# Cosine-weighted attention and a low-rank mixer: q of batch 3 transposed by DMA, the attention work of batches 3 to 7 in other slots, the last output chunk cut at column 384

## The chip, the core and the metric

The kernel runs on one core of a Trainium2 chip. A core has a matrix engine (PE, whose weight loads are shown as PEld), a vector engine (DVE), a scalar engine (ACT), GpSimd (POOL) and SyncE (SP), which here only issues DMAs. Each takes its instructions in program order and waits on semaphores for the others. The metric is the device time of one launch in microseconds (us), lower is better.

## The reference

There are 8 batches, 8 heads, 576 rows and 64 columns per head; the mixer has 512 columns, rank 32 and a hidden layer of 2048.

```python
def phi(x, c, s):                       # c, s: cos and sin of pi/2 * row / 576
    r = np.maximum(x, 0.0)
    return np.concatenate([r * c, r * s], axis=-1)
q_p = phi(q, cos_w, sin_w); k_p = phi(k, cos_w, sin_w)
kv = np.einsum('bhsf,bhsd->bhfd', k_p, v)
z = np.sum(k_p, axis=2)
num = np.einsum('bhsf,bhfd->bhsd', q_p, kv)
den = np.einsum('bhsf,bhf->bhs', q_p, z)[..., None] + 1e-06
x = (num / den)                         # heads side by side: 576 x 512 per batch
h = x.transpose(0, 2, 1) @ U @ V        # mixes the 576 rows, rank 32
u = x + h.transpose(0, 2, 1)
out = u + np.maximum(u @ w_ch1, 0.0) @ w_ch2
```

## The kernel before

**Rows.** The 576 rows of a batch are four chunks of 128 (c = 0 to 3) and a tail of 64 (c = 4). The tails of two batches share a tile of 128 rows, so batches go in pairs (0,1), (2,3), (4,5), (6,7). `ORD` is the order tail, 0, 1, 2, 3.

**Slots.** The order of all work is written out by hand. The big matmuls of a pair are 72 slots. Slots 0 to 15 are `g1_main` of the even batch (the first layer: four matmuls of 512 columns and one evacuation to `hid` on ACT, L475), 16 to 31 that of the odd batch, 32 to 35 `g1_tail`, and 36 to 71 `g2_part`: nine output chunks of four slots each, 16 matmuls per chunk, after which DVE adds `u` (L528, `o_sb`) and a store is issued. Pair 0 has slots 0 to 71, pair 1 has 72 to 143, pair 2 has 144 to 215, pair 3 has 216 to 287. After slot i come the small pieces that are listed for i. A slot of four 512-column matmuls takes 0.865 us on PE, as the chain of waits shows ("1.73 PE g_ps L466 x8").

**Attention of a batch**, planned by `attention_plan(b, w)` at offsets from w:

- `loads` of k, v and q, issued on SP. `kst` has two buffers; `vst`, `qst`, `k_p`, `q_p` and `q_pT` have one.
- `v_prep` casts v; `k_prep` and `q_prep` make the cos half and the sin half of the features of each chunk (L211 where ACT does it, L213 where DVE does it). The engines are arguments.
- q is transposed, by `qtr_unit` (eight PE transposes a chunk through PSUM, L262, then one copy) for batches 2 and 3, or by `qtr_dma` (three DMA transposes issued on SP, L275 and L280) for batches 4 to 7.
- `kv_unit` at w and w+2, `x_unit` at w+4 to w+12 (matmuls L339; DVE computes the reciprocal and the product, L296, L297, L349, and frees the only "X" buffer of PSUM), `A_unit` at w+14 (L365, cast on DVE), `u_unit` at w+16 to w+20 (L382, DVE add L383), and `utr_dma` (DMA transposes of u on SP, L401 and L407) at w+18 to w+21.

The windows are w = 40, 57, 88, 124, 160, 196 for batches 2 to 7. Batch b must be through before `g1_main` of its half-pair: slot 72 for batch 2, 88 for batch 3, 144, 160, 216, 232 for the others.

```python
p0 = -26 if b % 2 == 0 and b > 2 else -14
...
put(p0 + n, k_prep, c, (A_, A_) if b == 3 else (V_, V_))
```

Tile tags with two or three PSUM buffers ("o" 2, "g" 3) are lent to the small pieces by `spare`: "o" in the first 36 slots of a pair, where `g1` runs, "g" in the last 36.

**The last chunk** (pair 3, cc = 8) is cut into two halves of 256 columns in one PSUM tile, each with its own add and store on SP. Stores of the other pairs are issued on POOL.

Of the kernel before, what the change touches and what calls it, by code (L numbers as in the profile page):

```python
# [17 lines left out]
def kernel(  # L18
# [11 lines left out]
    nc = tc.nc  # L30

    B = 8
    H = 8
# [4 lines left out]
    DM = 512  # L38
    DH = 2048
    R = 32  # L40
    NJ = DH // P
    NPAIR = B // 2
# [19 lines left out]
    def alloc_k(b):  # L62
        kst[b] = pool.tile([P, H, 4, D], FP32, tag="kst", bufs=2, name="kst")
        kt[b] = pool.tile([P, H, D], FP32, tag="kt", bufs=2, name="kt")

    def alloc_v(b):
        vst[b] = pool.tile([P, H, 4, D], FP32, tag="vst", bufs=1, name="vst")
        vt[b] = pool.tile([P, H, D], FP32, tag="vt", bufs=1, name="vt")

    def alloc_q(b):  # L70
        qst[b] = pool.tile([P, H, 4, D], FP32, tag="qst", bufs=1, name="qst")
        qt[b] = pool.tile([P, H, D], FP32, tag="qt", bufs=1, name="qt")

    def load_main(dst, src, b, h0=0, h1=H, eng=None):
        (eng or nc.sync).dma_start(
            out=dst[:, h0:h1, :, :].rearrange("p h c d -> p h (c d)"),
            in_=src[b, h0:h1, 0:512, :].rearrange("h (p c) d -> p h (c d)", c=4),
        )

    def load_tail(dst, src, b, eng=None):  # L80
        (eng or nc.sync).dma_start(
            out=dst[tail(b), :, :],
            in_=src[b, :, 512:S, :].rearrange("h s d -> s h d"),
        )
# [23 lines left out]
    V_, A_, G_ = nc.vector, nc.scalar, nc.gpsimd  # L108
# [391 lines left out]
    def g2_part(pr, cc, part):  # L500

        last = pr == NPAIR - 1 and cc == 8
        if part == 0:
            o_ps[pr, cc] = ps.tile([P, DM], FP32, tag="o", bufs=2, name="o_ps")
        o = o_ps[pr, cc]
        if cc == 4:
            b, lhs, c, u = None, hid_tl[pr], 0, u_tl[pr]
        else:
            b, c = (2 * pr, cc) if cc < 4 else (2 * pr + 1, cc - 5)
            lhs, u = hid[b], u_bf[b][:, c, :]  # L510

        if last:
            cols, js = slice(part // 2 * 256, part // 2 * 256 + 256), part % 2 * 8
            js = range(js, js + 8)
        else:
            cols, js = slice(0, DM), range(part * 4, part * 4 + 4)
        for j in js:
            nc.tensor.matmul(  # L518
                out=o[:, cols],
                lhsT=lhs[:, j, c * P : c * P + P],  # L520
                rhs=w2_bf[:, j, cols],
                start=(j == 0),
                stop=(j == NJ - 1),
            )
        if js[-1] < NJ - 1:
            return
        o_sb = pool.tile([P, DM], FP32, tag="o_sb", bufs=3, name="o_sb")
        nc.vector.tensor_tensor(  # L528
            out=o_sb[:, cols], in0=u[:, cols], in1=o[:, cols], op=ALU.add
        )  # L530
        eng = nc.sync if pr == NPAIR - 1 else nc.gpsimd
        if cc == 4:
            for i in range(2):
                eng.dma_start(
                    out=out[2 * pr + i, 512:S, :], in_=o_sb[i * TS : i * TS + TS, :]
                )
        else:
            eng.dma_start(  # L538
                out=out[b, 0:512, cols].rearrange("(p c) n -> p c n", c=4)[:, c, :],
                in_=o_sb[:, cols],  # L540
            )


    def loads(b, eng):
        def kk():
            alloc_k(b)
            load_tail(kt[b], k, b, eng)
            load_main(kst[b], k, b, eng=eng)

        def vv():  # L550
            alloc_v(b)
            load_tail(vt[b], v, b, eng)
            load_main(vst[b], v, b, eng=eng)

        def qq():
            alloc_q(b)
            load_tail(qt[b], q, b, eng)
            load_main(qst[b], q, b, eng=eng)

        return kk, vv, qq  # L560

    ORD = (4, 0, 1, 2, 3)

    Q_BY_DMA = (4, 5, 6, 7)

    def spare(at):

        return ("o", 2) if at % 72 < 36 else ("g", 3)

    def attention_plan(b, w):  # L570

        plan = []

        def put(at, f, *a, tag=False):
            if tag:
                a = a + spare(w + at)
            plan.append((w + at, lambda: f(b, *a)))

        p0 = -26 if b % 2 == 0 and b > 2 else -14
        for n, c in enumerate(ORD):  # L580
            at = {2: -21, 3: -20}.get(b, p0 - 1)
            put(at + n, v_prep, 0, H, (c,), (G_ if b == 2 else A_,))
        for n, c in enumerate(ORD):
            put(p0 + n, k_prep, c, (A_, A_) if b == 3 else (V_, V_))
            if b in (2, 3):
                put(p0 + n, q_prep, c, (V_, A_))
            else:
                put(p0 + n, q_prep, c, (A_, None))
                put(p0 + n + 1, q_prep, c, (None, A_))
            if b not in Q_BY_DMA:  # L590
                ev = A_ if b in (2, 3) and n % 2 == 0 else V_
                put(-9 + 2 * n, qtr_unit, c, 0, H, ev)
        lo = {2: (-20, -15, -7), 3: (-13, -12, -7)}.get(b)
        if b in Q_BY_DMA:
            q0 = {4: -9, 6: -14}.get(b, p0 + 4)
            for n, (c0, c1) in enumerate(((0, 2), (2, 4), (4, 5))):
                put(q0 + 2 * n, qtr_dma, c0, c1)
            lo = (q0 + 5, q0 + 6, q0 + 7)
        put(0, kv_unit, 0, tag=True)
        put(2, kv_unit, 1, tag=True)  # L600
        for n, c in enumerate(range(5) if b in Q_BY_DMA else ORD):
            put(4 + 2 * n, x_unit, c, "X", 1)
        for n, c in enumerate(ORD):
            put(16 + n, u_unit, c, tag=True)
        put(14, A_unit, tag=True)
        if b % 2 == 1:
            put(18, utr_dma, 4, 5)
        put(19, utr_dma, 0, 2)
        put(21, utr_dma, 2, 4)
        if b + 1 < B:  # L610
            for at, t in zip(lo, loads(b + 1, nc.sync)):
                plan.append((w + at, t))
        return plan


# [120 lines left out]
    for pr in range(NPAIR):  # L736
        e, o = 2 * pr, 2 * pr + 1
        slots += [
            (lambda: None) if pr == 0 and 8 <= j < 13 else lambda j=j, e=e: g1_main(e, j)
            for j in range(NJ)  # L740
        ]
        slots += [lambda j=j, o=o: g1_main(o, j) for j in range(NJ)]
        slots += [lambda j=j, pr=pr: g1_tail(pr, j) for j in range(4)]
        slots += [
            lambda cc=cc, p=p, pr=pr: g2_part(pr, cc, p) for cc in range(9) for p in range(4)
        ]
# [3 lines left out]
    def put(at, thunk):  # L750
        todo.setdefault(at, []).append(thunk)
# [3 lines left out]
        put(18 + n, lambda b=b, c=c: u_unit(b, c, *spare(18)))  # L755
    for n, t in enumerate(loads(2, nc.sync)):
        put((11, 12, 12)[n], t)
    for b, w in ((2, 40), (3, 57), (4, 88), (5, 124), (6, 160), (7, 196)):
        for at, t in attention_plan(b, w):
            put(at, t)  # L760
    for i, s in enumerate(slots):
        s()
# [32 lines left out]
```

## Time and profile before

| | |
|---|---|
| median of 6 runs | 331.53 us (330.36 to 333.31) |
| the profiled execution: its time, its span | 330.84 us, 329.1 us |
| PE busy | 313.9 us, 95% of the span |
| ACT, DVE, POOL busy | 163.4, 151.9, 30.4 us |
| PE busy from 86 to 92 us | 3.49 of 6 us |
| PE busy from 110 to 116 us | 4.39 of 6 us |
| TensorE clock granted | 1.00 throughout |
| DMA | 50.73 MB, 154 GB/s in the mean |

A matmul's end in the trace is modelled and a running stream overlaps, so the distance between starts says more than the busy time: 216 ns for 512 columns. Where a group has one instruction fewer than the code issues (x7 for x8), its record is missing; the time is not. The stall ahead of a matmul is thus its start, less the start before it, less what the earlier one takes.

### The profile page before, as it was taken

How to read it: one execution, taken by the hardware profiler on the slowest of the kernel's cores; microseconds unless marked ns; L12 is line 12 of the kernel's file. 1: busy time of each engine (PE TensorE's matmuls, PEld its weight loads, DVE VectorE, ACT ScalarE, POOL GpSimd, SP SyncE). 2: the span in 40 equal slices, each digit the busy share in tenths (PEclk: the TensorE clock that was granted, in tenths of full speed). 3: DMA queues.
4: the chain of work that ended last, by engine and by line, in shares of the span. 5: the costliest groups of instructions: out<-in, count | busy, mean ns of one | idle time of the engine just before them, and what ended most of it. 6: DMA issues, size and time to landing. Idle time of an engine off the chain costs nothing.

```text
span 329.1 us, 5804 instructions
## 1 busy us (share of the span) xinstructions
PE 313.9 (95%) x2393; PEld 169.4 (51%) x2422; DVE 151.9 (46%) x334; ACT 163.4 (50%) x272; POOL 30.4 (9%) x61
## 2 busy tenths in 40 slices
PE   8899799999789799999999999999999999999995
PEld 3665654575455344556455444556455444464443
DVE  6779645825557851255626940345626610001211
ACT  3839655877719136555901866557700067650000
POOL 1314203001010100000111100000112000000000
PEclk9999999999999999999999999999999999999999
DMA  7999999877334118951499389702552230001131
GB/s 242 305 272 265 196 269 336 248 239 234 103 120 124 57 57 196 260 186 31 112 235 358 131 216 244 258 2 53 149 136 66 80 96 2 0 2 64 64 98 64
DMA packets 79053, 50.73 MB, mean 154 GB/s; under 512 B 47187, under 2 KB 76243, under 8 KB 79027
## 3 DMA queue, kind: packets, MB, share of 16 engines
q1 hardware_dynamic: 72594, 39.09, 42.1%
q0 software_dynamic: 6432, 11.27, 13.7%
q8 instruction: 19, 0.31, 0.4%
q14 instruction: 8, 0.06, 0.1%
HBM read 36.86 MB, written 9.44 MB: 141 GB/s over the span
## 4 chain that ended last, share of the span: by engine, by line
PE 66%; DVE 5%; issue 1%; ACT 1%; DVEq 0%
PE o_ps L518 30%; PE g_ps L466 25%; PE gt_ps L486 3%; PE va_ps L382 2%; PE kv_ps L245 2%; PE x_ps L339 2%; DVE k_p L213 2%; PE a_ps L365 2%; DVE o_sb L528 1%; PE t_ps L262 1%; DVE k_tl L213 1%; DVE rec L297 0%; ACT k_p L211 0%; DVE x_bf L349 0%; DVE rec L296 0%
## 5 line engine op out<-in xcount | busy, mean ns | idle before, releaser
L466 PE MATMUL g_ps<-uT,w_bf 128*128 128x512 bf16 x512 | 118.5, 379 | 0.1
L518 PE MATMUL o_ps<-w_bf,hid 128*128 128x512 bf16 (+1 forms) x510 | 116.3, 372 | 1.4 <-DVE o_sb L528 0.5
L475 ACT ACTIVATE hid<-g_ps 128x512 bf16<-128x512 f32 x128 | 76.2, 596 | 82.8 <-PE g_ps L466 82.7
L518 PEld LDWEIGHTS <-hid 128*128 128x128 bf16 x528 | 50.0, 98 | 53.5 <-issue 1.6
L466 PEld LDWEIGHTS <-w_bf 128*128 128x128 bf16 x512 | 48.5, 98 | 54.3
L528 DVE TENSOR_TENSOR o_sb<-u_bf,o_ps 128x512 f32<-128x512 bf16 (+1 forms) x33 | 22.1, 669 | 67.8 <-PE o_ps L518 67.7
L538 POOL DMA_DIRECT2D out_dram<-o_sb x24 | 13.4, 558 | 177.3 <-DVE o_sb L528 160.2
L383 DVE TENSOR_TENSOR u_bf<-x_bf,va_ps 128x512 bf16<-128x512 bf16 x32 | 21.9, 687 | 10.2 <-PE va_ps L382 9.4
L105 DVE CAST kv<-kv_ps 128x260 bf16<-128x260 f32 x14 | 6.0, 429 | 37.2 <-PE kv_ps L245 37.2
L211 ACT ACTIVATE q_p<-qst,sinw 128x512 bf16<-128x512 f32 x29 | 20.4, 710 | 4.4 <-DMA qst<-in_q_dram 4.4
L349 DVE TENSOR_TENSOR x_bf<-x_ps,rec 128x512 bf16<-128x512 f32 x24 | 16.6, 692 | 0.8
L103 ACT ACTIVATE v_ext<-vst 128x512 bf16<-128x512 f32 (+2 forms) x23 | 14.8, 653 | 2.9 <-DMA vst<-in_v_dram 2.8
L486 PE MATMUL gt_ps<-uT_tl,w_bf 128*128 128x128 bf16 x256 | 16.1, 219 | 0.0
L486 PEld LDWEIGHTS <-w_bf 128*128 128x128 bf16 x256 | 15.1, 98 | 1.4
L518 PE MATMUL o_ps<-w_bf,hid_tl 128*128 128x512 bf16 x62 | 15.0, 379 | 0.1
L382 PE MATMUL va_ps<-A_sb,V_bf 128*128 128x512 bf16 x37 | 14.0, 379 | 0.6 <-DVE A_sb L105 0.5
L245 PEld LDWEIGHTS <-k_p 128*128 128x128 bf16 x256 | 11.3, 97 | 5.1 <-ACT k_p L211 2.0
L172 PE MATMUL w_ps<-zero 128*128 128x512 bf16 x37 | 11.8, 459 | 1.9 <-DVE halfpi L142 1.2
L245 PE MATMUL kv_ps<-v_ext,k_p 128*128 128x65 bf16 x256 | 12.1, 193 | 1.6 <-DVE v_ext L105 1.5
L339 PEld LDWEIGHTS <-q_pT 128*128 128x128 bf16 x192 | 9.1, 98 | 8.2 <-DVE x_bf L349 1.6
L213 DVE TENSOR_SCALAR k_p<-kst,cosw 128x512 bf16<-128x512 f32 x28 | 13.1, 484 | 0.1
L296 DVE TENSOR_SCALAR rec<-x_ps 128x8 f32<-128x8 f32 (+1 forms) x30 | 4.9, 165 | 17.0 <-PE x_ps L339 16.9
(100 smaller groups left out, 261.2 us busy)
## 6 DMA issues: line engine op xcount, KB each, us to landing
qst<-in_q_dram SPq DMA_DIRECT2D x8, 1024.0 KB, 8.6
kst<-in_k_dram SPq DMA_DIRECT2D x8, 1024.0 KB, 7.3
vst<-in_v_dram SPq DMA_DIRECT2D x6, 1024.0 KB, 9.2
out_dram<-o_sb POOLq DMA_DIRECT2D x24, 256.0 KB, 2.8
w_bf<-in_moe_w_ch_dram POOLq DMA_DIRECT2D x8, 512.0 KB, 10.1
vst<-in_v_dram SPq DMA_DIRECT2D x4, 512.0 KB, 7.5
out_dram<-o_sb SPq DMA_DIRECT2D x7, 256.0 KB, 2.3
qt<-in_q_dram SPq DMA_DIRECT2D x8, 128.0 KB, 8.3
```

The lines of the kernel that those rows point to most:

```text
L211: nc.scalar.activation(out=o, in_=i, func=AF.Relu, bias=0.0, scale=w)
L213: eng.tensor_scalar(out=o, in0=i, scalar1=0.0, scalar2=w, op0=ALU.max, op1=ALU.mult)
L245: nc.tensor.matmul(out=acc[:, i, :], lhsT=k_p[b][:, c, h, :] if c < 4 else k_tl[:, h, :], rhs=vx[:, c, h, :], start=(c == 0), stop=(c == 4),)
L339: nc.tensor.matmul(out=acc[:, g, i * E : i * E + E], lhsT=qT_of(b, c, h), rhs=kv_sb[b][:, h, :], start=True, stop=True,)
L349: nc.vector.tensor_tensor(out=x_of(b, c, rows).rearrange("p (g i d) -> p g i d", g=2, d=D), in0=view[:, :, :, 0:D], in1=rec[rows].unsqueez ...
L382: nc.tensor.matmul(out=va, lhsT=V_bf[:, c, :], rhs=A_sb[b], start=True, stop=True)
L383: nc.vector.tensor_tensor(out=u_bf[b][:, c, :] if c < 4 else u_tl[b // 2][rows, :], in0=x_of(b, c, rows), in1=va[rows, :], op=ALU.add,)
L466: nc.tensor.matmul(out=g_ps.rearrange("p (c t) -> p c t", c=4), lhsT=w1_bf[:, d, j * P : j * P + P], rhs=uT[b][:, :, d, :], start=(d == 0) ...
L475: nc.scalar.activation(out=hid[b][:, j, :], in_=g_ps, func=AF.Relu, bias=0.0, scale=1.0)
L486: nc.tensor.matmul(out=g_ps[:, jj, :], lhsT=w1_bf[:, d, j * P : j * P + P], rhs=uT_tl[pr][:, d, :], start=(d == 0), stop=(d == 3),)
L518: nc.tensor.matmul(out=o[:, cols], lhsT=lhs[:, j, c * P : c * P + P], rhs=w2_bf[:, j, cols], start=(j == 0), stop=(j == NJ - 1),)
L528: nc.vector.tensor_tensor(out=o_sb[:, cols], in0=u[:, cols], in1=o[:, cols], op=ALU.add)
```

## The change

`attention_plan` takes its placements from a table, `PLAN`: w, start and engine of `v_prep`, start and engines of `k_prep`, start of `q_prep`, start of the DMA transposes of q (or "tensor"), and the places at which the loads of the next batch are issued. Batch 2 stays as it was. For batch 3 the transposes of q go from PE to DMA. Batches 3 to 7 get w = 60, 98, 128, 164, 200. Batch 4 gets `v_prep` on POOL, `k_prep` on ACT 35 slots ahead of its w, `q_prep` on DVE; for batches 5 to 7 every offset stays and w moves by four slots. The last chunk becomes 384 columns (three parts) and 128 columns (one part), the latter in a PSUM tile of its own, with its store issued on ACT.

```diff
     def g2_part(pr, cc, part):
         last = pr == NPAIR - 1 and cc == 8
-        if part == 0:
+        if part == 0 or last and part == 3:
             o_ps[pr, cc] = ps.tile([P, DM], FP32, tag="o", bufs=2, name="o_ps")
...
         if last:
-            cols, js = slice(part // 2 * 256, part // 2 * 256 + 256), part % 2 * 8
-            js = range(js, js + 8)
+            cols = slice(0, 384) if part < 3 else slice(384, DM)
+            js = (range(0, 5), range(5, 10), range(10, NJ), range(NJ))[part]
...
-        eng = nc.sync if pr == NPAIR - 1 else nc.gpsimd
+        eng = nc.gpsimd if pr < NPAIR - 1 else nc.scalar if part == 3 and last else nc.sync
...
+    KA, KV = ((A_, A_),) * 5, ((V_, V_),) * 5
+    PLAN = {
+        2: (40, -21, G_, -14, KV, -14, "tensor", (-20, -15, -7)),
+        3: (60, -20, A_, -10, KA[:2] + ((V_, A_),) * 3, -15, -9, (-16, 2, 3)),
+        4: (98, -10, G_, -35, KA, -18, -12, (-7, -6, -5)),
+        5: (128, -15, A_, -14, KV, -14, -10, (-5, -4, -3)),
+        6: (164, -27, A_, -26, KV, -26, -14, (-9, -8, -7)),
+        7: (200, -15, A_, -14, KV, -14, -10, ()),
+    }
...
+        w, v_at, v_eng, k_at, k_engs, q_at, qtr, lo = PLAN[b]
...
-        p0 = -26 if b % 2 == 0 and b > 2 else -14
         for n, c in enumerate(ORD):
-            at = {2: -21, 3: -20}.get(b, p0 - 1)
-            put(at + n, v_prep, 0, H, (c,), (G_ if b == 2 else A_,))
+            put(v_at + n, v_prep, 0, H, (c,), (v_eng,))
         for n, c in enumerate(ORD):
-            put(p0 + n, k_prep, c, (A_, A_) if b == 3 else (V_, V_))
+            put(k_at + n, k_prep, c, k_engs[n])
             if b in (2, 3):
-                put(p0 + n, q_prep, c, (V_, A_))
+                put(q_at + n, q_prep, c, (V_, A_))
+            elif b == 4:
+                put(q_at + n, q_prep, c, (V_, V_))
             else:
-                put(p0 + n, q_prep, c, (A_, None))
-                put(p0 + n + 1, q_prep, c, (None, A_))
-            if b not in Q_BY_DMA:
-                ev = A_ if b in (2, 3) and n % 2 == 0 else V_
-                put(-9 + 2 * n, qtr_unit, c, 0, H, ev)
-        lo = {2: (-20, -15, -7), 3: (-13, -12, -7)}.get(b)
-        if b in Q_BY_DMA:
-            q0 = {4: -9, 6: -14}.get(b, p0 + 4)
+                put(q_at + n, q_prep, c, (A_, None))
+                put(q_at + n + 1, q_prep, c, (None, A_))
+            if qtr == "tensor":
+                put(-9 + 2 * n, qtr_unit, c, 0, H, A_ if n % 2 == 0 else V_)
+        if qtr != "tensor":
             for n, (c0, c1) in enumerate(((0, 2), (2, 4), (4, 5))):
-                put(q0 + 2 * n, qtr_dma, c0, c1)
-            lo = (q0 + 5, q0 + 6, q0 + 7)
+                put(qtr + 2 * n, qtr_dma, c0, c1)
...
-    for b, w in ((2, 40), (3, 57), (4, 88), (5, 124), (6, 160), (7, 196)):
-        for at, t in attention_plan(b, w):
+    for b in range(2, B):
+        for at, t in attention_plan(b):
             put(at, t)
```

More of the change, by code (lines that the diff above doesn't have):

```diff
@@ L562, with attention_plan @@
     ORD = (4, 0, 1, 2, 3)
-    Q_BY_DMA = (4, 5, 6, 7)
     def spare(at):
         return ("o", 2) if at % 72 < 36 else ("g", 3)
-    def attention_plan(b, w):
+    KA, KV = ((A_, A_),) * 5, ((V_, V_),) * 5
[7 more added lines that the diff above has]
+    }
+    def attention_plan(b):
         plan = []
+        w, v_at, v_eng, k_at, k_engs, q_at, qtr, lo = PLAN[b]
         def put(at, f, *a, tag=False):
@@ L577, in put @@
             plan.append((w + at, lambda: f(b, *a)))
-        p0 = -26 if b % 2 == 0 and b > 2 else -14
         for n, c in enumerate(ORD):
-            at = {2: -21, 3: -20}.get(b, p0 - 1)
-            put(at + n, v_prep, 0, H, (c,), (G_ if b == 2 else A_,))
+            put(v_at + n, v_prep, 0, H, (c,), (v_eng,))
         for n, c in enumerate(ORD):
-            put(p0 + n, k_prep, c, (A_, A_) if b == 3 else (V_, V_))
+            put(k_at + n, k_prep, c, k_engs[n])
             if b in (2, 3):
-                put(p0 + n, q_prep, c, (V_, A_))
-            else:
-                put(p0 + n, q_prep, c, (A_, None))
-                put(p0 + n + 1, q_prep, c, (None, A_))
-            if b not in Q_BY_DMA:
-                ev = A_ if b in (2, 3) and n % 2 == 0 else V_
-                put(-9 + 2 * n, qtr_unit, c, 0, H, ev)
-        lo = {2: (-20, -15, -7), 3: (-13, -12, -7)}.get(b)
-        if b in Q_BY_DMA:
-            q0 = {4: -9, 6: -14}.get(b, p0 + 4)
+                put(q_at + n, q_prep, c, (V_, A_))
+            elif b == 4:
+                put(q_at + n, q_prep, c, (V_, V_))
+            else:
+                put(q_at + n, q_prep, c, (A_, None))
[3 more added lines that the diff above has]
+        if qtr != "tensor":
             for n, (c0, c1) in enumerate(((0, 2), (2, 4), (4, 5))):
-                put(q0 + 2 * n, qtr_dma, c0, c1)
-            lo = (q0 + 5, q0 + 6, q0 + 7)
+                put(qtr + 2 * n, qtr_dma, c0, c1)
         put(0, kv_unit, 0, tag=True)
         put(2, kv_unit, 1, tag=True)
-        for n, c in enumerate(range(5) if b in Q_BY_DMA else ORD):
+        for n, c in enumerate(ORD if qtr == "tensor" else range(5)):
             put(4 + 2 * n, x_unit, c, "X", 1)
@@ L609, in attention_plan @@
         put(21, utr_dma, 2, 4)
-        if b + 1 < B:
-            for at, t in zip(lo, loads(b + 1, nc.sync)):
-                plan.append((w + at, t))
+        for at, t in zip(lo, loads(b + 1, nc.sync) if lo else ()):
+            plan.append((w + at, t))
         return plan
```

## The prediction

> **What bounds the kernel now.** I read the page first: PE is busy 95% of the span, and of the 40 slices only the first five, three near 82 to 115 us and the last one dip.
>
> ```profile
> PE 313.9 (95%) x2393; PEld 169.4 (51%) x2422; DVE 151.9 (46%) x334; ACT 163.4 (50%) x272; POOL 30.4 (9%) x61
> PE   8899799999789799999999999999999999999995
> ```
>
> So PE's stream is the kernel, and a gain is either fewer matmuls or less waiting between them. Next the chain of waits, which leaves PE from 86 to 88, at 91, and from 105 to 114 us:
>
> ```profile
> 86.01 1.22 ACT k_p L211 x2
> 87.23 0.61 ACT q_p L211
> 87.85 0.49 ACT q_tlT L103
> 88.38 0.61 PE t_ps L262 x8
> ...
> 91.08 0.70 DVE q_pT L105
> 91.82 0.61 PE t_ps L262 x8
> ...
> 111.09 1.67 DVE k_p L213 x4
> 112.75 0.59 DVE o_sb L528
> ```
>
> ACT and DVE copy the transposes of batch 3 out of the single "T" buffer late, because feature work stands before the copies in their queues; later DVE frees the single "X" buffer late, because `k_prep` of batch 4 stands between the products of batch 3. PE's timeline has the sizes:
>
> ```profile
> 86.36 0.42 PE L339 MATMUL x_ps<-kv,q_pT 128*128 128x65 bf16 x8
> 88.38 0.61 PE L262 MATMUL t_ps<-ident,q_p 128*128 128x128 bf16 x8 [1.60 <-ACT q_tlT L103]
> ...
> 111.50 1.89 PE L518 MATMUL o_ps<-w_bf,hid 128*128 128x512 bf16 x8
> 114.53 0.42 PE L339 MATMUL x_ps<-kv,q_pT 128*128 128x65 bf16 x8 [1.15 <-DVE x_bf L349]
> ...
> 323.74 1.91 PE L518 MATMUL o_ps<-w_bf,hid 128*128 128x256 bf16 x16 [0.51 <-DVE o_sb L528]
> ```
>
> A stall is the start minus the start before it minus what that group takes (0.26 us for eight of L339, 1.73 for eight of 512 columns, both from the chain). 88.38-86.36-0.26 = 1.76; likewise 1.01 at 91.82, 0.34 at 108.61, 0.62 at 111.23, and 114.53-111.50-1.73 = 1.30. Sum: **5.03 us**. One more, 0.48 at 187.23, where `u_unit` of batch 5 waits for the cast of `A_sb`.
>
> **What the Trainium skill says.** "TensorE: Matmul & The Clock Gate", Back-to-back issue gap, gives some 81 ns per matmul for a stream of weight loads and 128-column matmuls and 56 ns for an isolated one. Here 16 of `gt_ps` take 0.89 us and eight transposes 0.45: 56 ns, weight loads included, and I use that. "PSUM — Partial Sum Buffer", PSUM bank collisions, wants engines kept apart by bank, not by address; the trace agrees: at 323.74 the second half waits for DVE's read of other columns of the same tile. "DMA: Bandwidth & Descriptors", Issuing engines are not separate DMA queues, says a store from another engine saves only sequencer time; no run shown has one from ACT. "SBUF — State Buffer", Who interferes with whom, says a DVE instruction with two SBUF inputs contends with GpSimd's reads; the trace before doesn't decide that.
>
> **The change, part by part.**
>
> *Batch 3 transposed by DMA.* Removed: 5 x 8 transposes, 5 x 0.45 = -2.24 us of PE, and the stalls behind "T", 1.76 + 1.01 = -2.77. ACT also loses three copies (two of 1.0 us, one 0.58), DVE two of 0.69. Added: three transposes on SP, 1.4 to 2.3 us each to issue, landing 3.8 to 5.3 after. q features are done on DVE near 86.7 us (its queue worked through from 79 us: products 1.07, features 0.40, adds 0.6 each), so SP issues from 85 to 90 and the last lands by 95; the first `x_unit` needs them at 102. Hidden. `x_unit` of batch 2 beside `q_prep` of batch 3 waits 0.12 at most, once: +0.12.
>
> *Batch 4's k to ACT, q and v elsewhere.* DVE has only products and adds left while batch 3's `x_unit` runs (2 x 0.865 + 0.26 = 2.0 us per unit against 1.07 + 0.3): -0.34-0.62-1.30 = -2.26. Ten k halves on ACT, 6.1 us from 100.2 (when `kv_unit` of batch 3 releases `k_p`), end at 106.4; the first `hid` of slot 72 comes at 110. Five casts on POOL (612 ns each) have 20 slots; were DVE shut out all that time, 3.1 us would be spread over units with 0.6 spare each, so I take nothing, at most +1. Ten q halves on DVE (4 us) lie in slots 80 to 84, where DVE has only the `u` adds, which stand first.
>
> *Batch 3 three slots later.* A uT transpose lands 2.7 us after issue; with the last issue near 120.0 (its `u` add ends then) it is in at 122.7 and slot 88 starts at 125.3. Nothing, with 2.6 us in hand (5 before: 127.5 against 132.5).
>
> *Batches 5 to 7 four slots later, batch 4 ten.* The output chunks recur every four slots, so the 0.48 us wait of batch 5 stays. Its `u_unit`s now fall on slots 144 to 148 and take "o" (2 buffers) for "g" (3); the second waits for the add of chunk 8: about +0.26. New is a meeting: `u_unit` of batch 4 (114 to 118) now shares its slots with `k_prep` of batch 5 on DVE. With T the start of the first of these `u` matmuls, DVE needs 0.65 + 0.8 per slot and one add, so u of c = 1 is done at T+4.4 and of c = 3 at T+7.3. SP is in order: uT transpose (T+4.4), q transpose of batch 5, uT transpose (T+7.3), two q transposes, at 1.25 to 2.3 us each: `loads` of batch 6 begin at T+12.3. In the trace before they begin at 168.10:
>
> ```profile
> 168.10 0.69 SPq L81 DMA_DIRECT2D kt<-in_k_dram  x1
> ...
> 173.80 2.52 SPq L75 DMA_DIRECT2D qst<-in_q_dram  x1
> ```
>
> q lands 10.9 us after its issue, at 184.7, and ACT, already waiting for these loads, finishes features at 190.8, just ahead of the next `hid`:
>
> ```profile
> 180.70 0.63 ACT L103 ACTIVATE v_ext<-vst 128x512 bf16<-128x512 f32 x1 [2.79 <-DMA vst<-in_v_dram]
> ...
> 190.14 0.71 ACT L211 ACTIVATE q_p<-qst,sinw 128x512 bf16<-128x512 f32 x1
> 191.74 0.60 ACT L475 ACTIVATE hid<-g_ps 128x512 bf16<-128x512 f32 x1 [0.90 <-PE g_ps L466]
> ```
>
> That is 22.7 us from first issue to free ACT; after, T+35.0, and the first `hid` of pair 2 is out of PSUM at T+35.6. PE starts slot 119 at T+4.5; from 119 to 144 took 26.5 us before, 0.86 of it `u_unit`s that now come later, so slot 144 starts at T+30.2 and slot 147, which needs the buffer of slot 144 ("g" has three), at T+30.2+3x1.08+0.26 = 33.7. **New stall: +1.85 us**, between 0 (loads land 2 us sooner) and +4 (2 us later). Behind it ACT needs 0.5 to 0.6 per `hid` against 0.865 per slot and catches up.
>
> *Last chunk.* PE issues the same 16 x 512 columns. The 128-column part has its own tile, and chunk 7's buffer was free 2 us before: the gap goes, 323.74 minus the end of the first half's stream, -0.68 (the 0.51 shown counts from a modelled end). The last add covers 128 columns: 0.42 for 256 and 0.69 for 512 give 0.285, -0.13. The 384-column add (0.55) ends within the last part's 0.89. The store: the last one before took 1.8 us from issue to landing on SP; from ACT, with nothing before or behind it, I take the same, -0.3 to +0.5 at the ends. Sum -0.81.
>
> *Sum*: -2.24-2.77-2.26+0.12+0.26+1.85-0.81 = **-5.85 us**. The profiled 330.84 becomes 325.0; it lies 0.7 below the median, 331.53, which becomes 325.7.
>
> **The rivals.**
>
> *The loads are not late*, since DVE or SP needs less than I added up. For: ACT had 0.9 us spare at 191.74. Against: ACT waited 2.8 us on v there already. Then +1.85 goes: 323.8.
>
> *A removed wait returns at slot 88*: uT of batch 3 late by 5 us, where 2.6 are in hand. For: nothing else was moved so near its deadline. Against: SP has nothing else to issue then. +2.4: 328.1.
>
> *Slower: SP's in-order queue decides.* Place: slot 147. Each us by which q of batch 6 lands later than I worked out is a us of PE. For: transposes and 3.4 MB of loads now share SP behind `u_unit`; the GB/s row has its highest value, 358, in that stretch. Against: the same bytes, only shifted. It costs more than 5.85+1.66, the bound of "slower", once q lands 7.5 us later than assumed; with its 10.9 us doubled, 336.6.
>
> **How the numbers follow.** Forecast (stall at 147 of 0.5 to 4) 0.60; loads not late 0.24; slot 88, or another return of that size, 0.11; SP decides 0.05. I allow 0.7 for where the median falls among runs that differ by up to 2.95. The range reaches from the second case less that, 323.1, to just over the slot-88 case and the forecast with a stall of 4 us (327.9), 328.5. Some 0.5% (1.66 us) is what a measurement of this kernel can tell from no change: faster 0.91, same 0.04, slower 0.05.
>
> **What would show it.** Right: no PE transpose (L262) after slot 39, so 120 of the 160 are left; PE near 6 of 6 us from 80 to 115; no gap ahead of the 128-column matmuls; one gap of 1 to 3 us at the fourth `g1_main` of pair 2, released by an ACT `hid` that follows a q feature. Wrong: PE waiting at slot 88 for uT, at slot 64 for `q_pT`, gaps between the `x_unit`s of batch 3, or a last store that takes over 2.3 us.

## The result, and the profile after

The changed kernel takes 328.97 us in the median of 16 executions (326.11 to 331.62), the one before 331.76 (35 executions); the ratio is 0.990, 95% interval 0.9874 to 0.9927. That is 2.8 to 3.3 us less, where 5.85 was forecast. The profiled execution took 326.92 us, its span is 325.1. (The ratios leave out executions over 1.5% above the fastest of their kernel; the counts of clock below keep them.)

The page after: busy time of PE, its share per slice, and the granted clock, which the page before shows at 9 in all slices.

```profile
PE 312.5 (96%) x2356; PEld 167.1 (51%) x2382; DVE 151.8 (47%) x335; ACT 156.5 (48%) x261; POOL 33.2 (10%) x66
PE   8799799999999999999999979999999999999996
PEclk9999799999999999999999999999999999999999
```

The dips near 82 to 115 us are filled. Slice 24 is new, and so is a 7 in the fifth slice of the clock. PE's timeline where batch 3's `x_unit`s had waited 0.34, 0.62 and 1.30 us:

```profile
103.94 0.42 PE L339 MATMUL x_ps<-kv,q_pT 128*128 128x65 bf16 x8
104.20 1.89 PE L518 MATMUL o_ps<-w_bf,hid 128*128 128x512 bf16 x7
105.93 0.42 PE L339 MATMUL x_ps<-kv,q_pT 128*128 128x65 bf16 x8
106.19 1.89 PE L518 MATMUL o_ps<-w_bf,hid 128*128 128x512 bf16 x8
107.91 0.42 PE L339 MATMUL x_ps<-kv,q_pT 128*128 128x65 bf16 x8
```

Every distance is 0.26 or 1.73 us: no wait. The chain of waits leads through the new dip; its first line starts when SP issues the load of q of batch 6:

```profile
173.79 7.70 DMA qst<-in_q_dram
...
186.67 3.06 ACT q_p L211 x5
189.73 0.49 ACT hid L475
```

PE's timeline at the same place:

```profile
188.07 0.38 PE L382 MATMUL va_ps<-A_sb,V_bf 128*128 128x512 bf16 x1
190.26 1.02 PE L466 MATMUL g_ps<-uT,w_bf 128*128 128x512 bf16 x4 [1.82 <-ACT hid L475]
```

v and q of batch 6 land late: ACT waits 3.30 us for v and, as its last wait, 1.06 for q. Their casts and features stand on ACT before the first `hid` of pair 2, and the fourth `g1_main` waits for that `hid`: a stall of 1.98 us (start 190.26, less 188.07 of the `u` matmul before, less 0.22, from unrounded times). The end of the kernel, in the timeline:

```profile
321.32 0.55 DVE L528 TENSOR_TENSOR o_sb<-u_bf,o_ps 128x384 f32<-128x384 bf16 x1 [1.91 <-PE o_ps L518]
322.21 0.29 DVE L528 TENSOR_TENSOR o_sb<-u_bf,o_ps 128x128 f32<-128x128 bf16 x1 [0.34 <-PE o_ps L518]
322.53 0.38 ACTq L538 DMA_DIRECT2D out_dram<-o_sb  x1
```

The matmuls run through without a gap, and the adds take what was interpolated (0.55 and 0.285).

**One measure that start and chip don't touch.** Up to slot 40 the two programs do the same work, but for three casts of batch 3 that move behind it. From the first `kv_unit` matmul of batch 2 (L245, at 75.29 before and 77.24 after) to the end of the span is 253.78 us before and 247.90 after: **-5.88 us**. The 1.95 that the profile after lost ahead of it lie in a stretch that no edit touches; from 36.21 to 39.62 us its granted clock is 0.50, which accounts for some 1.7 of them. I call this distance "from slot 40" below.

### The profile page after: what moved, and what is told of

The parts are those of the page before. It is cut to its first block, busy times and chain, and to the rows that moved or that the text cites. A ratio compares the mean times of both kernels' runs of the same rounds, so it can differ in the third digit from the quotient of the medians.

```text
span 325.1 us, 5735 instructions
## 1 busy us (share of the span) xinstructions
PE 312.5 (96%) x2356; PEld 167.1 (51%) x2382; DVE 151.8 (47%) x335; ACT 156.5 (48%) x261; POOL 33.2 (10%) x66
## 4 chain that ended last, share of the span: by engine, by line
PE 80%; DMA 9%; SPq 4%; ACT 3%; DVE 2%; issue 1%
PE o_ps L518 34%; PE g_ps L466 32%; DMA kt<-in_k_dram 5%; PE gt_ps L486 4%; DMA qst<-in_q_dram 2%; PE va_ps L382 2%; SPq L81 2%; PE kv_ps L245 2%; DMA vst<-in_v_dram 2%; PE x_ps L339 2%; PE a_ps L365 2%; SPq L75 2%; ACT q_p L211 2%; PE t_ps L262 1%; DVE k_p L213 1%
## 5 line engine op out<-in xcount | busy, mean ns | idle before, releaser
L466 PE MATMUL g_ps<-uT,w_bf 128*128 128x512 bf16 x512 | 120.3, 382 | 2.0 <-ACT hid L475 1.8
L518 PE MATMUL o_ps<-w_bf,hid 128*128 128x512 bf16 (+2 forms) x513 | 117.7, 372 | 0.8
L518 PEld LDWEIGHTS <-hid 128*128 128x128 bf16 x528 | 48.9, 98 | 51.9 <-issue 0.3
L528 DVE TENSOR_TENSOR o_sb<-u_bf,o_ps 128x512 f32<-128x512 bf16 (+2 forms) x33 | 22.0, 668 | 55.4 <-PE o_ps L518 55.2
L211 ACT ACTIVATE q_p<-qst,sinw 128x512 bf16<-128x512 f32 x25 | 17.3, 711 | 3.7 <-DMA qst<-in_q_dram 3.7
L349 DVE TENSOR_TENSOR x_bf<-x_ps,rec 128x512 bf16<-128x512 f32 x24 | 16.6, 691 | 0.8
L486 PE MATMUL gt_ps<-uT_tl,w_bf 128*128 128x128 bf16 x256 | 15.8, 219 | 0.0
L245 PEld LDWEIGHTS <-k_p 128*128 128x128 bf16 x256 | 11.2, 97 | 6.2 <-ACT k_p L211 2.0
L245 PE MATMUL kv_ps<-v_ext,k_p 128*128 128x65 bf16 x256 | 12.0, 193 | 2.5 <-DVE v_ext L105 2.5
L103 ACT ACTIVATE v_ext<-vst 128x512 bf16<-128x512 f32 (+2 forms) x19 | 12.2, 659 | 3.6 <-DMA vst<-in_v_dram 3.5
L103 ACT ACTIVATE v_ext<-vt 64x512 bf16<-64x512 f32 (+1 forms) x7 | 3.7, 534 | 19.5 <-DMA vt<-in_v_dram 19.4
```

The costliest lines, as they stand in the source:

```text
L103: nc.scalar.activation(out=o, in_=i, func=AF.Copy, bias=0.0, scale=1.0)
L211: nc.scalar.activation(out=o, in_=i, func=AF.Relu, bias=0.0, scale=w)
L245: nc.tensor.matmul(out=acc[:, i, :], lhsT=k_p[b][:, c, h, :] if c < 4 else k_tl[:, h, :], rhs=vx[:, c, h, :], start=(c == 0), stop=(c == 4),)
L349: nc.vector.tensor_tensor(out=x_of(b, c, rows).rearrange("p (g i d) -> p g i d", g=2, d=D), in0=view[:, :, :, 0:D], in1=rec[rows].unsqueez ...
L466: nc.tensor.matmul(out=g_ps.rearrange("p (c t) -> p c t", c=4), lhsT=w1_bf[:, d, j * P : j * P + P], rhs=uT[b][:, :, d, :], start=(d == 0) ...
L486: nc.tensor.matmul(out=g_ps[:, jj, :], lhsT=w1_bf[:, d, j * P : j * P + P], rhs=uT_tl[pr][:, d, :], start=(d == 0), stop=(d == 3),)
```

## The experiments

Unless said otherwise each is an edit of the changed kernel, run beside the kernel before on one chip, on which before has a median of 333.1 to 333.2. The second run of the later k features and the run with q of batch 5 on PE were on another chip, where before has 332.87.

**The changed kernel again, and the one before again.** No edit.

> The changed kernel itself, unedited, beside the kernel before on one chip, to compare at an equal mean clock. Theory (the trace's -5.9 us from slot 40 on is the change, and what the medians show less is clock): 5 to 6.5 us less than before among executions of the same mean clock, and a lower mean clock on average than before. Rival (the first 40 us got slower too): 3 to 4 us less at an equal clock.

> The kernel before, unedited, for a second profile. Theory (clock drops follow the stalls of PE): where its mean clock is under 1, the low stretch lies at the start, before 45 us, or behind one of the stalls at 88 to 92 and 108 to 115 us. Rival (drops fall anywhere): elsewhere too.

Changed: 331.51 us (6 executions), ratio 0.9874 (0.9797 to 0.9951). Before: 333.23 (20 executions), ratio 0.9987 (0.9963 to 1.0011); from slot 40 it takes 253.76, the first profile within 0.02, with the same five stalls and a clock of 1.00. The changed kernel takes 251.03 from slot 40 this time, 3.13 more than in its first profile. PE's timeline shows where:

```profile
189.43 0.38 PE L382 MATMUL va_ps<-A_sb,V_bf 128*128 128x512 bf16 x1
193.07 1.02 PE L466 MATMUL g_ps<-uT,w_bf 128*128 128x512 bf16 x4 [3.26 <-ACT hid L475]
193.93 0.38 PE L382 MATMUL va_ps<-A_sb,V_bf 128*128 128x512 bf16 x1
194.15 1.66 PE L466 MATMUL g_ps<-uT,w_bf 128*128 128x512 bf16 x4
```

The stall is 3.42 us here (q of batch 6 landed 30.8 us after the first `u` matmul of batch 4, in place of 29.4), and one microsecond after it four matmuls take 1.66 us in place of 1.02. So the stall is dearer than its length: 1.44 us of the 3.13 are the longer stall, the other 1.7 the slower matmuls behind it. The windows of three profiles show when this happens. A row gives a stretch, its length, the busy time (and the instructions) of PE, PEld, DVE, ACT and POOL, the granted clock, the DMA share and GB/s. First this second profile of the changed kernel, with its stall of 3.42 us:

```profile
190.99:194.40 3.41, 1.33 (x7) 0.62 (x7) 0.05 (x1) 3.26 (x7) 0.00 (x0) 1.00 0.35 77
194.40:197.81 3.41, 3.41 (x10) 1.22 (x9) 1.32 (x2) 0.93 (x2) 0.00 (x0) 0.50 0.00 0
```

Then the run with k of batch 4 on DVE (below), whose stall there is 2.28 us:

```profile
188.11:191.53 3.42, 1.30 (x7) 0.52 (x6) 1.42 (x3) 3.42 (x7) 0.16 (x1) 1.00 0.60 165
191.53:194.94 3.41, 3.41 (x10) 1.17 (x9) 0.69 (x1) 1.30 (x3) 0.00 (x0) 0.50 0.12 27
```

And the run with q of batch 3 on PE (below), whose stall is 3.55 us and which has no low stretch behind it:

```profile
190.70:194.11 3.41, 1.63 (x7) 0.58 (x6) 2.34 (x4) 3.41 (x7) 0.54 (x1) 1.00 0.38 115
194.11:197.53 3.42, 1.67 (x8) 0.77 (x8) 0.39 (x1) 3.26 (x6) 0.00 (x0) 1.00 0.34 77
197.53:200.94 3.41, 3.41 (x18) 1.56 (x16) 0.99 (x2) 1.92 (x4) 0.00 (x0) 1.00 0.28 65
```

In each of the twelve profiles the changes of the clock lie whole multiples of 3.413 us apart (in this second profile at 37.39, 40.80, 194.40 and 197.81; from 37.39 to 194.40 it is 46 times 3.413), a grid whose place differs from one execution to the next. What goes with a low stretch is not how long the stall is but how much of it falls into one window of that grid. Behind slot 40, up to the output's last chunk, the clock fell to 0.50 after the three windows in which PE was idle for 2.08, 2.09 and 2.12 us, and after none with less: 1.78 and 1.75 (the 3.55 us stall, cut in two by the grid), 1.51, 1.51, 1.38, 1.16, and 1.37 for the stalls behind "T" in the kernel before. (Once it stayed at 0.50 for a second window.) Ahead of slot 40 six of seven low stretches follow windows with 1.89 us of idle time or more, but one follows a window with 1.39, so this is not the whole rule. It is read from the traces; no edit moved a stall against the grid.

By mean granted clock, executions and median us:

| | 0.998 and over | 0.993 to 0.995 | 0.990 and under |
|---|---|---|---|
| before (one chip, 83) | 28: 332.0 | 49: 333.5 | 6: 335.5 |
| changed (16 + 6) | 4: 326.2 | 8: 328.8 | 10: 331.6 |
| early loads, below (6) | 2: 324.2 | 4: 326.5 | none |
| early loads, k of batch 6 on ACT, below (6) | 5: 323.4 | 1: 324.2 | none |

One low stretch, 3.41 us at half speed, loses 1.7 us, which is 0.005 of the mean clock over 330 us. So, by this estimate, the columns are executions with no low stretch, with one, and with two or more.

At an equal clock the table puts the change at 3.9 to 5.8 us, but its second row takes in the first measurement, where before is some 1.3 us faster than on the one chip. On that chip there are six executions of the changed kernel: one at full clock, 327.14 against about 332.2 (5.1 less), one at 0.995, 329.82 against 333.5 (3.7 less), and four at 0.990 and under, 332.2 against 335.5 (3.3 less). One execution bears the expectation of 5 to 6.5 out; the others lie at the rival's 3 to 4, so the rival is not excluded. The lower clock on average is there: on that chip 4 of 6 executions have lost a second stretch, against 6 of 83 before. Of the changed kernel and its edits, 27 of 69 executions of those that have the stall are at 0.990 and under, and none of the 14 of the three edits below that remove it (an execution at 0.852, below, is left out). The theory that before's drops follow its stalls got no case: neither of its profiles has a drop.

**k features of batch 5 after the u adds of batch 4, twice.**

```diff
-        5: (128, -15, A_, -14, KV, -14, -10, (-5, -4, -3)),
+        5: (128, -15, A_, -9, KV, -14, -10, (-5, -4, -3)),
```

> The changed kernel with k_prep of batch 5 five slots later (offset -9 for -14), so that DVE does the u adds of batch 4 first. Theory 1 (DVE delays u, u delays the transposes on SP, they delay the loads of batch 6, ACT is late for the hid of slot 144): loads of batch 6 begin 2.7 us sooner after the first u matmul of batch 4 (13.4 us in the changed kernel), and the stall of 1.98 us at the fourth g1_main of pair 2 falls below 0.2; 2.0 us less at an equal clock. Rival 1 (the landing of the loads is bound by what the DMA engines can move, not by when SP issues): the stall stays above 1.5. Theory 2 (that stall is also where the matrix clock drops in some executions): the median falls by clearly more than 2.0, to below 326. Rival 2 (the clock drops come from the start, which no edit touches): the median falls by 2.0, to 327.0, and runs with a mean clock of 0.99 stay as common.

> The kernel with k_prep of batch 5 five slots later once more, for a second profile and more executions. Theory (moving k_prep helps only by what SP can pass on, some 0.4 us in the first profile): the stall at the fourth g1_main of pair 2 is between 1.5 and 3.5 us again. Rival (the first profile was a disturbed one and the edit does remove the stall): below 0.5.

326.47 us (6 executions, ratio 0.9792, 0.9749 to 0.9835) and, on the other chip, 326.65 (4 executions, one of them 364.5 us at a clock of 0.852; ratio 0.9819, 0.9773 to 0.9865). The stall is not gone: 3.43 us in the first profile, which is of the slowest execution of its six (332.49), and 1.55 in the second.

```profile
164.68 2.46 SPq L280 DMA_TRANSPOSE q_tlT<-q_tl  x1
167.19 0.61 SPq L81 DMA_DIRECT2D kt<-in_k_dram  x1
```

These are SP's rows of the second. The first transpose is issued 1.5 us sooner (3.29 after the first `u` matmul of batch 4, in place of 4.81), but the last one now takes 2.46 us to issue in place of 1.25, and the loads begin at 12.8 (13.1 in the first profile) in place of 13.5 and 14.1. So of the 2.7 us I expected, 0.4 to 1.3 came through, and the order of DVE's work is not enough to remove the stall. The median is 5.0 us below the changed kernel's on the same chip (331.51) all the same: at full clock it is 325.73 against one execution at 327.14, and fewer executions are at 0.990 and under, one of six against four of six. How much of that is a shorter stall in the executions without a profile is not known.

**q of batch 5 transposed on PE.**

```diff
-        5: (128, -15, A_, -14, KV, -14, -10, (-5, -4, -3)),
+        5: (128, -15, A_, -14, KV, -14, "tensor", (-5, -4, -3)),
```

> The changed kernel with q of batch 5 transposed on PE (slots 119 to 127), so that three DMA transposes fewer stand ahead of the loads of batch 6. Theory (the transposes hold SP and the DMA engines): the loads begin near 9.2 us after the first u matmul of batch 4 (13.5 and 14.1 in the two profiles of the changed kernel), q lands near 22 (29.4 and 30.8), 12 to 13 us from first issue to landing in place of 16, and PE has no stall at the fourth g1_main of pair 2; PE itself works 2.2 us more. Rival (the loads are slow by their own bytes): 16 us from first issue to landing again, q lands at 25.

327.54 us (2 executions on the other chip, ratio 0.9846, 0.9793 to 0.9898). Loads begin at 10.0 and q lands at 25.9: 16.0 us from first issue to landing, against 15.8 and 16.6 in the changed kernel and 17.5 and 16.0 above. The rival holds: the 3.5 MB of loads took about as long without these transposes ahead of them (221 GB/s in the mean), and the transposes cost by holding SP until the loads may begin. ("tensor" also puts the tail first among this batch's `x_unit`s; the same goes for batch 3 below.) With a start 4 us sooner the stall at the fourth `g1_main` is gone. From slot 40: 247.91, the same as the changed kernel, 2.2 of PE work for 2.0 of stall.

**Loads of k and v of batch 6 ahead of those transposes.**

```diff
-        5: (128, -15, A_, -14, KV, -14, -10, (-5, -4, -3)),
+        5: (128, -15, A_, -14, KV, -14, -10, (-20, -12, -3)),
```

> The changed kernel with the loads of k and v of batch 6 issued at slots 108 and 116, ahead of the transposes, and q's after them as before. Theory (the loads of batch 6 come late because the transposes before them on the same queue fill the DMA engines; what counts is the bytes and transposes ahead, not when SP issues): q of batch 6 lands near 23 us after the first u matmul of batch 4 (29.4 in the changed kernel, 30.6 where only k_prep of batch 5 was moved), the stall at the fourth g1_main of pair 2 is below 0.2 us, 2.0 to 3.5 us less at an equal clock, and the clock drop after it is gone. Rival (k_prep of batch 5 on DVE is the cause): the stall stays above 1.5.

325.73 us, ratio 0.9761 (0.971 to 0.9813). Only q is left behind the transposes:

```profile
166.46 1.22 SPq L280 DMA_TRANSPOSE q_tlT<-q_tl  x1
168.41 0.62 SPq L75 DMA_DIRECT2D qst<-in_q_dram  x1
```

q lands 22.4 us after the first `u` matmul of batch 4 (23 expected), 6.9 sooner than in the changed kernel: 4.5 of these are an earlier issue (at 15.0 in place of 19.5), 2.4 a shorter way to landing. So when SP issues does count, other than the theory had it. The stall is gone; from slot 40: 245.92, 1.98 less than the changed kernel, which is the stall of its first profile to the last digit. And none of the 6 executions has a clock of 0.99 or less. Since `k_prep` of batch 5 stands where the change put it, the rival falls.

**And k features of batch 6 on ACT, its `v_prep` and `k_prep` seven slots sooner.**

```diff
-        6: (164, -27, A_, -26, KV, -26, -14, (-9, -8, -7)),
+        6: (164, -34, A_, -33, KA, -26, -14, (-9, -8, -7)),
```

> The same, and k_prep of batch 6 on ACT at slots 131 to 135 in place of DVE at 138 to 142. Theory: the two waits for A_sb and for the add of chunk 8 (0.49 and 0.31 us in the changed kernel) go as well, 0.8 us less than with the early loads alone. Rival (ACT has no room for ten more features): the stall at the fourth g1_main of pair 2 comes back, over 1 us.

323.54 us (322.85 to 324.19), ratio 0.9696 (0.9652 to 0.9739): the best version found, below both kernels. From slot 40: 244.99, another 0.93 less (0.8 expected, the two waits of 0.49 and 0.31), and PE has no gap over 0.24 us from slot 36 to the end:

```profile
PE   8899799999999999999999999999999999999996
```

**Parts undone: q of batch 3 on PE, k of batch 4 on DVE, the last chunk in halves.**

```diff
-        3: (60, -20, A_, -10, KA[:2] + ((V_, A_),) * 3, -15, -9, (-16, 2, 3)),
+        3: (60, -20, A_, -10, KA[:2] + ((V_, A_),) * 3, -15, "tensor", (-16, 2, 3)),
```

> The changed kernel with q of batch 3 transposed on PE again (slots 51 to 59), all features where the change put them. Theory (the stalls behind the T buffer came from features queued ahead of the copies, so the new slots alone remove most of them): 2.24 us of PE work comes back and at most 0.5 us of stalls, +2.2 to +2.7 at an equal clock. Rival (the single T buffer makes PE wait wherever the features stand): the two stalls of 2.8 us come back too, +5.0.

331.66 us (20 executions), ratio 0.9951 (0.9927 to 0.9976). From slot 40: 251.97, 4.07 more than the changed kernel's first profile; its stall at the fourth `g1_main` is 3.55, 1.57 more, which leaves +2.5. There is no gap at the five transposes; two of them, the first with its neighbours:

```profile
90.05 1.02 PE L518 MATMUL o_ps<-w_bf,hid 128*128 128x512 bf16 x4
90.91 0.61 PE L262 MATMUL t_ps<-ident,q_tl 128*128 128x128 bf16 x8
91.35 1.03 PE L518 MATMUL o_ps<-w_bf,hid_tl 128*128 128x512 bf16 x4
...
93.34 0.61 PE L262 MATMUL t_ps<-ident,q_p 128*128 128x128 bf16 x8
```

The distances are 0.86 and 0.44 us, what the matmuls take. 2.24 us of work come back, and the stalls of 2.77 do not. So the new slots of the features are enough to remove these, without the DMA transposes.

```diff
-        4: (98, -10, G_, -35, KA, -18, -12, (-7, -6, -5)),
+        4: (98, -10, G_, -35, KV, -18, -12, (-7, -6, -5)),
```

> The changed kernel with k_prep of batch 4 on DVE (slots 63 to 67) instead of ACT. Theory (the 2.26 us of stalls at x_unit of batch 3 are DVE's k features queued between the products): the gaps between the x_units return, +1.5 to +2.5 us at an equal clock. Rival (ORD against plain order, or the later slots, removed them): below +0.5.

332.88 us (12 executions), ratio 0.9991 (0.9961 to 1.0021). The stalls at `x_unit` of batch 3 are back, in PE's timeline:

```profile
107.27 0.42 PE L339 MATMUL x_ps<-kv,q_pT 128*128 128x65 bf16 x8 [0.48 <-DVE x_bf L349]
110.40 0.43 PE L339 MATMUL x_ps<-kv,q_pT 128*128 128x65 bf16 x8 [0.98 <-DVE x_bf L349]
```

0.64 and 1.14 us, +1.78 in the range expected. Its whole gain over before vanished in these executions, since 10 of 12 had a clock of 0.99 or less; in its profile the clock drops behind the stall at the fourth `g1_main`.

```diff
-        if part == 0 or last and part == 3:
+        if part == 0:
...
-            cols = slice(0, 384) if part < 3 else slice(384, DM)
-            js = (range(0, 5), range(5, 10), range(10, NJ), range(NJ))[part]
+            cols, js = slice(part // 2 * 256, part // 2 * 256 + 256), part % 2 * 8
+            js = range(js, js + 8)
...
-        eng = nc.gpsimd if pr < NPAIR - 1 else nc.scalar if part == 3 and last else nc.sync
+        eng = nc.gpsimd if pr < NPAIR - 1 else nc.sync
```

> The changed kernel with the last chunk as two halves of 256 columns in one PSUM tile, both stores on SP. Theory: +0.8 us, of it 0.68 as a gap ahead of the last sixteen matmuls and 0.13 in the last add. Rival (the store from ACT with 512-byte rows costs what the add saves): +0.5 or less.

330.09 us (6 executions), ratio 0.991 (0.9873 to 0.9947), too wide for 0.8 us. The profile decides: 249.74 from slot 40, 1.84 more, of which the stall at the fourth `g1_main` (2.90) has 0.92; the other 0.92 is the end, where the gap is back:

```profile
322.68 1.91 PE L518 MATMUL o_ps<-w_bf,hid 128*128 128x256 bf16 x16 [0.51 <-DVE o_sb L528]
```

## Why the prediction was right or wrong

- **What bounds the kernel** was right: every term was a gap or a matmul on PE, and the terms add up. From slot 40 the sum was -5.85 and the first profile has -5.88. That it is this close is in part luck: single terms are off by up to 0.13 us, and the other profile of the same kernel has 3.13 less gain. In the medians 2.8 to 3.3 us came. By the ratio that is 328.2 beside the 331.53 that the forecast started from, inside the range of 323.1 to 328.5, but near the end that was there for a long stall or a wait at slot 88. That it also held what the clock took is luck.
- **Batch 3's q: -2.24 and -2.77** are right as sums, but the second was put down to the DMA transposes alone. The stalls came from features queued before the copies, as the prediction itself says ahead of its sum; with PE transposes in the new slots they stay away too. DMA transposes with the features in their old slots were not tried. SP issued these transposes later than worked out, from 90.45 to 97.74 us with the last landing at 100.41 (85 to 90 and 95; 1.95 of this is the later start), and they were still hidden: the first of batch 3's `x_unit`s starts at 104.11.
- **Batch 4's k on ACT: -2.26** is right: no gap in the profile after, 1.78 of it back when k goes back to DVE. The five casts on POOL delayed no `x_unit`.
- **Slot 88** was met, as worked out: the last uT of batch 3 lands at 124.85 us and slot 88 starts 2.6 later. The rival of a wait returning there has no trace in the profile.
- **The new stall, +1.85**, was right in its place and its mechanism from ACT on, and 1.98 in the first profile. But its size is not a constant: seven profiles with it show 1.55 to 3.55 us, as q of batch 6 lands 28.8 to 30.9 us after the first `u` matmul of batch 4. From profile to profile the stall grows by about as much as q lands later, as the slower rival had it. The bounds of 0 to 4 held these; the middle was low for most (and 35.6 less 33.7, the prediction's own figures, is 1.9). That the first profile came so near is in part luck: the loads began at 13.5 us in place of 12.3, and from their first issue to free ACT took 21.9 us in place of 22.7. The step that named its cause was too simple: I made DVE's backlog the cause, and moving it passed on 0.4 to 1.3 of 2.7 us, because the issue of the last transpose on SP then took 2.46 and 2.99 us in place of 1.25 and 2.22.
- **What was left out** is the step that missed the median: no term for the granted clock. The page before showed 9 in all slices, so I priced a stall at its length. The Trainium skill, "TensorE: Matmul & The Clock Gate", Part 1, says that the clock is halved after an idle window of about 3.4 us that runs free of the kernel. The low stretches here do come on a grid of 3.41 us, at a clock of 0.50, but the window need not be idle throughout: PE was busy for 1.30 to 1.33 of the 3.41 us ahead of the three. So stalls of 2.28, 3.42 and 3.43 us were followed by a low stretch, and those of 1.55, 1.98, 2.90 and 3.55, cut in two by the grid, were not; before's two stalls of 1.77 and 1.01 us left at most 1.37 us idle in one window. Without the stall none of 14 executions had the second drop; of the changed kernel's 22, 10 had. That removing the stall ends the second drop is shown as far as 14 executions go; the limit between 1.78 and 2.08 us of idle time is only read off.
- **The last chunk, -0.81**: 0.92 by the part undone, 0.67 of it the gap. The store from ACT landed 1.70 us after issue, as the one from SP did (1.83).
- **The slots up to 40**, taken as unchanged, are all but unchanged in work but not in time: kv of batch 2 starts at 75.3 to 77.4 us in the five profiles with no low stretch ahead of it and at 77.2 to 79.1 in the seven with one. 49 of before's 83 executions have a low stretch's loss in their mean clock too, so it does not come with the change alone; what sets the rest of the start was not tried.

## What to carry to other kernels

Where one in-order queue issues both transposes and loads, a load's landing is set by when its turn comes plus the time of the loads themselves (16 us for q, k and v of a batch here): issue loads whose buffers are already free ahead of work that has to wait, and look whose features, on which engine, stand in front of the first evacuation of the next stage. Price a stall on the matrix engine that can leave 2 us idle within one window of 3.41 at more than its length: here the clock was halved for the next 3.41 us, which cost another 1.7. Whether it comes is a matter of chance between executions, so count it over many. And compare profiles from a common instruction on, so that a variable start and a clock drop don't pass for the change.

## What the runs showed of the hardware that I had not expected

- A stall can cost a second time: after a window of 3.41 us in which PE was idle for 2.08 to 2.12, the granted clock was 0.50 for the next window (two in one profile). Where the grid cut a stall of 3.55 us into 1.78 and 1.75, nothing followed.
- The time that SP takes to issue a DMA transpose varies: the same tail transpose (batch 5) took 1.22 to 2.99 us across profiles, and the one issued before it 2.18 to 3.79. What sets it is not shown. An estimate that adds up the issue times of one profile can be low by a microsecond or more.
